# Linformer attention and gated FFN on one core: constants counted and transposed on VectorE instead of iotas on GpSimd, the broadcast library loaded behind the first loads

## The chip, the cores and the metric

One core of one Trainium2 chip. The metric is the device time of one execution in microseconds (us). Engines are called TensorE (PE in the profile), VectorE (DVE), ScalarE (ACT), Pool (GpSimd) and SP (SyncE). "PEld" is TensorE's weight load. The granted clock is the share of TensorE's full clock that the profile records as allowed; 0.5 is called the half clock below.

## The reference, cut to what matters

```python
k_proj = einsum('ks,bhsd->bhkd', E, k)            # B=8, H=8, S=1024, D=64, 64 projected keys
v_proj = einsum('ks,bhsd->bhkd', F, v)
attn   = softmax(q @ k_proj^T / 8)
x      = (attn @ v_proj), heads side by side      # 8192 x 512
out    = (sigmoid(x @ w_gate) * (x @ w_val)) @ w_out   # d_ff = 1536
```

Inputs are float32; the kernel loads all but E and F as bf16, casting in the DMA.

## The kernel before

Pool issues the large loads. The order of its work, with the iotas between the loads (shapes cut):

```python
def start_loads():
    # SP: E and F, 256 KB each
    load_k(0)                                    # Pool: K of batch 0, 1 MB written
    pool(iota(col_i), w=["col_i"]); pool(iota(row_i), w=["row_i"])
    load_q_half(0, 0); load_v(0)
    pool(iota(pat_i)); pool(iota(eight_i)); pool(iota(pat4_i))
    load_w(0); load_w(1); load_q_half(0, 1); load_w(2); load_w(3)

def constants():                                 # VectorE
    copy(col_f, col_i); copy(row_f, row_i)       # int32 -> float32
    identf = (col_f == row_f); ident = ...       # identity, float32 and bf16
    half, low, negm, dsel8, bsel8, bsel, dsel    # small masks, from col_i, row_i and the patterns
```

The head of the program, in TensorE's order. `busy(n)` are n filler matmuls that feed nothing. They are meant to keep the clock up; its mean was 1.0 in every run of before, but that the fillers do it is not shown.

```python
start_loads(); constants()
project_consts()              # transposes E and F with identf, 8 matmuls
busy(56)
project(0, 0, ...)            # K of batch 0 times E; waits for K
keep_k; turn_k(whole)
qt(0); qt(1); sc(0); sc(1); den()    # waits for q's first half; scores, exp, denominators
project(1, 1, ...)            # V of batch 0 times F; waits for V
keep_v; busy(8); bc(0); busy(4); xo(0); bc(1); xo(1); busy(10)   # xo: attention times V
load_q(1); load_k(1); load_v(1); load(wO)        # Pool: batch 1 and w_out
# then the dense FFN matmuls with the attention of the next batch in between;
# SP transposes q of batch 1 by four DMA transposes
```

Later (from batch 2 on), Pool spreads the reciprocals with `partition_broadcast`, which lies in another Pool library than iota: the trace of before has MODIFY_POOL_CONFIG at the first iota's line (2.33 us) and again at the broadcast's (110.5 us).

The softmax here doesn't subtract the row's maximum and nothing guards it: scores larger than these inputs give would overflow.

## Time and profile before

| | before |
|---|---|
| median of the first runs | 580.79 us (580.11 to 581.54, 4 runs) |
| all runs of before, over the study | 579.88 to 582.35 us |
| span of the profiled run | 578.0 us |
| TensorE busy | 555.5 us, 96% |
| first TensorE work | 15.48 us |
| first attention-times-V matmul (`xo`) | 30.37 us |
| dense FFN matmuls from | 33.46 us |

TensorE is near full use in all but the first 33 us, so the head is what can still be shortened. The prediction shows the lines that say so.

### The profile page before, as it was taken

Reading aid. Unit: us, or ns where it says so; the run is one execution under the profiler, and the core shown is the slowest. Engines: PE = TensorE matmul, PEld = TensorE weight load, DVE = VectorE, ACT = ScalarE, POOL = GpSimd, SP = SyncE. Lnnn points to the kernel's source line nnn. Section 1 sums busy time; section 2 is a strip of 40 time slices with the busy share of each in tenths; the row PEclk is TensorE's granted clock in tenths of the full one; section 3 lists DMA queues with packets and bytes.
Section 4 is the critical chain, followed back from the end, with each engine's and each line's share of the span. In section 5 each row is a group of like instructions: output and inputs, shape, how many; then the busy total and the mean of one; then the engine's idle time right before and its main releaser. Section 6 shows DMA issues by size and latency. Waiting matters only on the chain.

```text
span 578.0 us, 7834 instructions
## 1 busy us (share of the span) xinstructions
PE 555.5 (96%) x3110; PEld 252.1 (44%) x3110; DVE 246.4 (43%) x381; ACT 175.1 (30%) x317; POOL 101.5 (18%) x139
## 2 busy tenths in 40 slices
PE   0899999999999999999999999999999999999997
PEld 0644434544444444444444444444445444444443
DVE  0446355335443356235363354433562353633332
ACT  0355443352223422333223522234223332222220
POOL 1800010102600053000810026000520008000000
PEclk9999999999999999999999999999999999999999
DMA  6999979892576047650696125771311011100002
GB/s 109 160 203 200 186 125 194 150 195 58 108 148 119 37 65 134 127 90 36 111 173 104 44 57 108 148 119 37 75 56 45 21 38 38 37 36 19 36 37 91
DMA packets 74212, 56.01 MB, mean 97 GB/s; under 512 B 34528, under 2 KB 65760, under 8 KB 74176
## 3 DMA queue, kind: packets, MB, share of 16 engines
q0 software_dynamic: 31776, 29.89, 33.7%
q1 hardware_dynamic: 42400, 25.63, 17.5%
q8 instruction: 24, 0.39, 0.3%
q14 instruction: 12, 0.10, 0.1%
HBM read 60.29 MB, written 16.78 MB: 133 GB/s over the span
## 4 chain that ended last, share of the span: by engine, by line
PE 94%; issue 2%; DVE 2%; ACT 1%; POOL 0%; POOLq 0%; DVEq 0%
PE pF L218 85%; PE pA L218 9%; DVE rden L715 1%; ACT eT L222 0%; DVE xT L606 0%; ACT qT L222 0%; POOL KV L236 0%; DVE rden L553 0%; DVE vpD L464 0%; DVE identf L323 0%; DVE rhl L725 0%; DVE ost L878 0%; DVE hT L851 0%; DVE rhi L723 0%; ACT kp L222 0%
## 5 line engine op out<-in xcount | busy, mean ns | idle before, releaser
L851 DVE SCALAR_TENSOR_TENSOR hT<-sig,pF 128x512 bf16<-128x512 f32 x192 | 130.9, 685 | 203.3 <-PE pF L218 155.8
L222 ACT ACTIVATE sig<-pF 128x512 f32<-128x512 f32 x192 | 114.8, 599 | 315.9 <-PE pF L218 312.9
L218 PE MATMUL pF<-xT,wG 128*128 128x512 bf16 x768 | 198.6, 380 | 0.6 <-ACT rb L222 0.3
L218 PE MATMUL pF<-xT,wV 128*128 128x512 bf16 x768 | 198.2, 379 | 0.2 <-DVE xT L606 0.2
L218 PE MATMUL pF<-wO,hT 128*128 128x512 bf16 x720 | 165.4, 380 | 0.0
L218 PEld LDWEIGHTS pF<-xT,wV 128*128 128x128 bf16 x768 | 75.1, 98 | 90.9 <-issue 0.6
L218 PEld LDWEIGHTS pF<-xT,wG 128*128 128x128 bf16 x768 | 72.1, 98 | 94.2 <-issue 11.8
L760 POOL PARTITION_BROADCAST rb<-rrow x96 | 70.8, 798 | 219.3 <-DMA rrow<-rden 213.9
L218 PEld LDWEIGHTS pF<-wO,hT 128*128 128x128 bf16 x720 | 69.1, 98 | 87.3 <-issue 5.8
L878 DVE TENSOR_SCALAR ost<-pF 128x512 f32<-128x512 f32 x60 | 41.5, 691 | 94.0 <-PE pF L218 94.0
L222 ACT ACTIVATE eT<-pA 128x512 bf16<-128x512 f32 x63 | 32.7, 603 | 10.2 <-PE pA L218 10.2
L785 DVE TENSOR_TENSOR xT<-pA,rb 128x512 bf16<-128x512 f32 x56 | 34.7, 681 | 0.0
L715 DVE RECIPROCAL rden<-pA 128x128 f32<-128x128 f32 x28 | 23.7, 909 | 0.0
L236 POOL DMA_DIRECT2D KV<-in_k_dram x8 | 7.5, 937 | 82.4 <-PE pF L218 80.4
L236 POOL DMA_DIRECT2D KV<-in_v_dram x8 | 7.2, 895 | 75.0 <-PE pA L218 75.0
L218 PE MATMUL pA<-identf,EF 128*128 128x128 f32 x8 | 1.9, 421 | 15.5 <-DVE half L331 15.5
L218 PE MATMUL pA<-KV,EFT 128*64 128x256 bf16 x240 | 14.6, 274 | 0.0
L218 PEld LDWEIGHTS pA<-KV,EFT 128*64 128x64 bf16 x240 | 12.5, 110 | 3.1 <-issue 3.0
L222 ACT ACTIVATE kpd<-pA 128x512 bf16<-128x512 f32 x6 | 3.6, 597 | 28.4 <-PE pA L218 28.4
L218 PE MATMUL pA<-eT,vpD 64*64 64x512 bf16 (+1 forms) x136 | 10.4, 370 | 0.3 <-DVE vpD L464 0.3
L218 PE MATMUL pA<-qT,kpD 64*64 64x512 bf16 (+1 forms) x140 | 10.4, 367 | 0.3 <-ACT qT L222 0.3
L222 ACT ACTIVATE vpD<-pA 64x256 bf16<-64x256 f32 x28 | 10.5, 375 | 0.5
(74 smaller groups left out, 109.1 us busy)
## 6 DMA issues: line engine op xcount, KB each, us to landing
out_dram<-ost SPq DMA_DIRECT2D x64, 256.0 KB, 2.0
KV<-in_k_dram POOLq DMA_DIRECT2D x8, 1024.0 KB, 10.7
KV<-in_v_dram POOLq DMA_DIRECT2D x8, 1024.0 KB, 11.3
Qb<-in_q_dram POOLq DMA_DIRECT2D x7, 1024.0 KB, 15.2
wO<-in_moe_w_out_dram POOLq DMA_DIRECT2D x1, 1536.0 KB, 44.5
Qb<-in_q_dram POOLq DMA_DIRECT2D x2, 512.0 KB, 10.3
wG<-in_moe_w_gate_dram POOLq DMA_DIRECT2D x2, 512.0 KB, 18.3
wV<-in_moe_w_val_dram POOLq DMA_DIRECT2D x2, 512.0 KB, 20.1
```

The costliest lines, as they stand in the source:

```text
L218: return add("PE", lambda e: e.matmul(o, lhsT, rhs, **kw), r=r, x=[("bank", b)])
L222: return add("ACT", lambda e: e.activation(o, i, func, scale=scale), r=r, w=w, x=x)
L236: add("POOL", lambda e: e.dma_start(o, i), r=r, w=w, dma=sem)
L715: lambda e, cc=cc: e.reciprocal(rden[:, cc], bank[bk][:, cc]),
L760: lambda e, n=n, i=2 * rnd + c, j=j, parts=parts: e.partition_broadcast(rb[0:parts, n, :], rrow[32 * j : 32 * j + 1, i, :], channels=parts),
L785: lambda e, r=r, g=g, n=n, bk=bks[g]: e.tensor_tensor(xT[s][:, r, :, 256 * g : 256 * g + 256], bank[bk][:, :].rearrange("p (f c) -> p f c" ...
L851: lambda e: e.scalar_tensor_tensor(hT[blk % 2][:, m, :], sg[:, :], 1.0, bank[pv][:, :], ALU.add, ALU.mult,),
L878: lambda e: e.tensor_scalar(o[:, :], bank[pb][:, :], 0.5, None, op0=ALU.mult),
```

## The change

The intent is to have nothing of Pool's library code in front of the loads. Column numbers are built on VectorE by doubling (0, then +1, +2, +4 ...), row numbers by one transpose on VectorE of patterns 32 columns wide and adding 0, 32, 64, 96 (four memsets on Pool). The iotas go. The library with `partition_broadcast`, which was brought in by itself ahead of the first broadcast (at 110.5 us, the broadcast at 140.23), is asked for right behind the load of `wO`. The diff, cut to its core:

```diff
             load_k(0)                # four memsets of `quad` now stand ahead of it
-            pool(lambda e: e.iota(col_i[:, :], [[1, P]], channel_multiplier=0), w=["col_i"])
-            pool(lambda e: e.iota(row_i[:, :], [[1, 1]], channel_multiplier=1), w=["row_i"])
             load_q_half(0, 0)
             load_v(0)
-            ... (iotas of pat_i, eight_i, pat4_i)
 ...
         def constants():
-            dve(lambda e: e.tensor_copy(col_f[:, :], col_i[:, :]), ["col_i"], ["col_f"])
-            dve(lambda e: e.tensor_copy(row_f[:, :], row_i[:, :]), ["row_i"], ["row_f"])
+            dve(lambda e: e.memset(count[:, 0:1], 0.0), [], ["count"])
+            for i in range(7):
+                n = 1 << i
+                dve(tensor_scalar(count[:, n : 2 * n], count[:, 0:n], float(n), None, op0=ALU.add), ...)
+            dve(tensor_copy(pats[:, 0, :], count[:, 0:32]), ...)   # and three more patterns
+            dve(e.transpose(rows, pats), ["pats"], ["rows"])
+            dve(tensor_tensor(row_f, rows[:, 0, 0:1], quad, ALU.add), ...)
 ...   (dsel and dsel8 from twelve small pieces instead of four; bsel, bsel8, negm read `rows`)
         load(wO[:, :, :], moe_w_out.rearrange("(m p) c -> p m c", p=P), ["wO"], "wO")
+        spread_library = [ the first library that has InstPartitionBroadcast ]
+        pool(lambda e: e.load_library(spread_library))
```

## The prediction

> **What bounds the kernel now.** I read the page first, then the chain that ended last over the first 36 us, then the landing of each transfer, then the first use of each transferred tile. The page:
>
> ```profile
> span 578.0 us, 7834 instructions
> PE 555.5 (96%) x3110; PEld 252.1 (44%) x3110; DVE 246.4 (43%) x381; ACT 175.1 (30%) x317; POOL 101.5 (18%) x139
> PE   0899999999999999999999999999999999999997
> ```
>
> TensorE is busy in all but one slice of 14.45 us: the first reads 0. By TensorE's groups from 33 us to the end it idles about 1.4 us (0.9 of it one wait for `rhl`). So steady-state savings on other engines are worth nothing; the head before 33.46 us, where the dense FFN matmuls begin, is the only place this change can gain. The chain there (start, us, what):
>
> ```profile
> 1.24 1.01 POOL KV L236
> ...
> 2.33 0.03 POOLq L295
> ...
> 2.39 11.57 issue
> 13.96 0.24 POOL col_i L295
> ...
> 14.55 0.78 DVE identf L323
> ...
> 15.48 1.94 PE pA L218 x8
> 17.42 3.86 PE pF L218 x56
> 21.28 1.04 PE pA L218 x16
> ...
> 29.80 0.44 DVE vpD L464
> 30.23 0.14 issue
> 30.37 0.57 PE pA L218 x9
> ...
> 33.42 0.05 issue
> ```
>
> The reader should see a hole of 11.57 us between K's load and the first iota. The trace names the two Pool sequencer entries at 2.33 and 2.36 us MODIFY_POOL_CONFIG: the library with iota is being brought in. Everything after it in Pool's order waits too: the identity (so TensorE), but also every further load, because Pool issues them. The landings (issue time from Pool's timeline plus the last column, us from issue to landing):
>
> ```profile
> KV<-in_k_dram POOLq DMA_DIRECT2D x1, 1024.0 KB, 11.1
> EF<-in_F_dram SPq DMA_DIRECT2D x1, 256.0 KB, 4.2
> ...
> KV<-in_v_dram POOLq DMA_DIRECT2D x1, 1024.0 KB, 10.6
> ...
> wG<-in_moe_w_gate_dram POOLq DMA_DIRECT2D x1, 256.0 KB, 10.4
> ```
>
> F: 1.38+4.2 = 5.6 us. K: 1.24+11.1 = 12.35. First half of Q: 14.24+5.8 = 20.1. V: 15.33+10.6 = 25.9. First gate weights: 16.86+10.4 = 27.3. K sat landed for 8.9 us before its projection at 21.28.
>
> [...] The gap ends 1.6 us after K landed, so the load may also wait for the transfer under way; this profile cannot tell. [...] a q transpose issued at 50.00 us, beside the load stream, takes 11.9 us; the one at 72.24, when the stream is over, 3.0. [...]
>
> **The change, part by part.**
>
> *Five iotas and the library in front of them leave Pool.* 11.57 us of load, plus 0.23+0.12 us and some 0.65 us of later iotas in Pool's order. Added in front of K are four memsets; the four at 0.24 us start about 0.03 apart and last 0.10, so K issues some 0.15 us later: landing about 12.5. Pool's remaining issues (0.75 to 1.1 us each) follow at once: q's first half at about 2.4, wO, the last, near 14.5 instead of 26.33.
>
> *Constants on VectorE.* A small operation lasts 0.13 to 0.15 us (rows `half`, `low_i`); a dependent one starts about 0.04 us after its predecessor, estimated 0.18 per step. Memset plus seven doublings: 1.45; four patterns, which overlap: 0.5; [...] row_f 0.18; identf 0.78+0.12 to TensorE. Sum 3.5 us. VectorE can begin near 0.7 us (ScalarE's and SP's first work starts at 0.72), so the identity is ready at about 4.2, against 15.4. F lands at 5.6 and now starts TensorE. The rest (two halves, twelve `dsel` pieces at about 0.15, two `bsel` at 0.47) ends near 8.5, while the first denominators are due after 17. The later use of a pattern column for `negm` costs the same.
>
> *TensorE's head.* Transposes of E and F 5.6 to 7.5 us, 56 warming matmuls to 11.4, then K's projection waits for K: 12.5 instead of 21.28. That would be worth 8.8 us. But the wait now belongs to the transfers, and these gain less than the 11.9 us by which their issue moves: K's own stream was running until 12.35, so only the empty gap in the stream is saved. Once running, a quarter MB lands each 1.3 to 1.4 us (gate and value chunks at 27.3, 28.5, 30.95, 32.1 us; then 0.5 MB per 2.6). Behind K, q's half lands at 12.5+2.65 = 15.1, V at 15.1+5.3 = 20.4 (before: 25.9, so 5.5 earlier), first weights 21.8 and 23.1.
>
> K projection, copy, transposes of kp take 12.5 to 14.4; q's half lets its transposes begin at about 15.0 (23.19 before, 8.2 gained). Scores, exp, denominators end at 27.68-8.2 = 19.5. V's projection then waits for V: 20.4 instead of 27.59, ends 21.45; the two VectorE copies of vpD take 0.9, to 22.35; TensorE's fillers and first broadcast (29.36 to 30.09 before) end at about 22.6. So xo begins at about 22.65 instead of 30.37: 7.7 us gained. FFN weights (23.1) are there before it starts at 25.75.
>
> *Further down,* needs move by 7.7 and landings by 5.5, so each must have had 2.2 us in hand. Gate chunk 2 lands 30.95 for 36.79: kept. q's other half 34.7 for 38.5: kept. V of batch 1 62.0 for about 65.9, wO 70.8 for 74.8: kept. The tightest is q's fourth transpose for batch 1:
>
> ```profile
> 72.24 1.23 SPq L624 DMA_TRANSPOSE qT<-Qb  x1
> ...
> qT<-Qb SPq DMA_TRANSPOSE x1, 3.0
> ...
> 77.45 0.63 PE L218 MATMUL pA<-qT,kpD 64*64 64x512 bf16 x8
> ```
>
> It lands at 75.28; the second half of the matmuls at 77.45 uses it from about 77.7: 2.4 us in hand, 2.2 needed. I allow 0.1 us for a small stall.
>
> *The broadcast library.* Before, Pool loaded it by itself at 110.5 us (MODIFY_POOL_CONFIG, line 760), unseen ahead of the first broadcast at 140.23, which waited for a DMA. Now it starts near 15.5 us; Pool's next order is K of batch 2, at 75.98 before (bound by the transpose landing at 75.28). Even a 12 us load, or one that waits for the stream's end at 65 and takes some us more, costs that load a few us of the 19 between its landing (86.5) and its use at 105.3. Zero.
>
> Sum: -7.7 + 0.1 = -7.6; 581.43 - 7.6 = 573.8 us, 1.3% less.
>
> **The rivals.**
> 1. *Everything moves by the full hole.* TensorE's first work goes from 15.48 to 5.6: 9.9 us at most, time 571.5. Against it: K's landing at 12.35 is not moved by the change, and V's comes behind it. Only if K's stream is being slowed by the library load (142 GB/s in 4 to 12 us, against 207 later) does it come near.
> 2. *Transfers take the wait over completely.* If the stream gains only the empty stretch (12.35 to about 16.4, some 4 us plus the restart), or the transposes for batch 1 slip by interleaving differently, the gain is 5 to 6 us: 575.5 to 576.5. For it: 2.4 us in hand is little. Against it: they hang on the same stream and should move with it.
> 3. *The library load has only moved.* If loading behind the stream blocks Pool until the stream has drained and for 12 us after, K of batch 2 issues at about 77 instead of 70 and still has over 15 us. If it also held up transfers under way, the head would lose up to its own length: about 581. Against it: K landed during the first load, V of batch 3 around the second.
> 4. *VectorE's chain is the new start.* Twice my 3.5 us puts the identity at 7.7, first matmul 2.1 later, end of the fillers at 13.5: 1 us past K, and V's later wait absorbs most of it. About 574.5.
>
> **Range and chances.** The main claim, a hole replaced by transfers already measured, is firm; its size lies between the stream's 5.5 and the compute's 8.8. Runs of before spread 1.4 us. So 573.8, from 571.3 to 576.6. Faster by over 2% would need 11.6 us, more than the 9.9 that the landing of F allows: 2%. Slower by over 2% needs a stall of 19 us that nothing here suggests: 1%.
>
> **What would show it.** Right: no empty stretch on Pool between K's and q's issue; first TensorE work at 5.5 to 6; K projection at 12 to 13, released by the K transfer; V's projection at 20 to 20.8, released by V; dense matmuls from about 25.7; after that the same busy TensorE. Wrong, and in which step: identity after 5.6 us (VectorE's chain); K landing clearly off 12.5 (rival 1 or a slower stream); TensorE idle near 66 to 70 us for qT, or near 57 for KV (rival 2); the load of K for batch 2 after 90 us (rival 3)[...].

Passages are cut: one was the term for the transpose in VectorE's chain; the chain's 3.5 us were summed with it, and the terms that are left come to 3.03. The forecast's own sum, 7.6 us gained and 573.8 us, rests on V's landing, not on the identity.

## The result, and the profile after

The changed kernel takes 572.83 us (median of 4 runs, 572.16 to 573.38) against 580.79. The ratio is 0.9862, 95% interval 0.9843 to 0.9881. Ratios here are the mean time of one kernel's fast runs over that of the other's of the same rounds, so not quite the ratio of the medians that are quoted. That is 1.4% faster, far clear of noise. The prediction was 573.8 us.

The page of the changed kernel; compare its first TensorE slices (0 and 8 before):

```profile
span 571.1 us, 7787 instructions
...
PE   5799999999999999999999999999999999999997
```

The timeline of the changed kernel's head: start, us, engine, line, operation, and in brackets the idle time before it and what ended it.

```profile
0.72 0.56 POOL L288 MEMSET quad<- 32x1 f32 x4 [0.29 <-POOLq L981]
1.34 1.02 POOL L228 DMA_DIRECT2D KV<-in_k_dram  x1
2.36 0.88 POOL L228 DMA_DIRECT2D Qb<-in_q_dram  x1
3.23 0.88 POOL L228 DMA_DIRECT2D KV<-in_v_dram  x1
3.35 0.31 DVE L334 STREAM_TRANSPOSE rows<-pats 128x128 f32<-128x128 f32 x1
3.90 0.29 DVE L348 TENSOR_SCALAR identf<-count,row_f 128x128 f32<-128x128 f32 x1
5.54 1.94 PE L210 MATMUL pA<-identf,EF 128*128 128x128 f32 x8 [5.54 <-DMA EF<-in_F_dram]
7.27 5.16 PE L210 MATMUL pF<-ident 128*128 128x128 bf16 x56
13.38 1.06 PE L210 MATMUL pA<-KV,EFT 128*64 128x256 bf16 x16 [0.94 <-DMA KV<-in_k_dram]
16.03 1.07 PE L210 MATMUL pF<-ident,Qb 128*128 128x128 bf16 x16 [0.67 <-DMA Qb<-in_q_dram]
21.13 1.06 PE L210 MATMUL pF<-KV,EFT 128*64 128x256 bf16 x16 [0.56 <-DMA KV<-in_v_dram]
23.33 0.41 PE L210 MATMUL pA<-eT,vpD 64*64 64x256 bf16 x8
```

The hole in Pool is gone: q follows K at once. The identity is ready at 4.19 us and TensorE's first work waits for F. From there three steps of the head are each released by a transfer in this profile: K's projection, q's transposes and V's projection. The transfers have taken over the wait. (In the repeat, `after_again`, K landed at 12.09 us and its projection waited until 12.54 for the end of the 56 fillers instead.) Their landings, from the list of DMA issues of the changed kernel (last column: us from issue to landing):

```profile
KV<-in_k_dram POOLq DMA_DIRECT2D x1, 1024.0 KB, 12.0
...
Qb<-in_q_dram POOLq DMA_DIRECT2D x1, 512.0 KB, 13.6
...
KV<-in_v_dram POOLq DMA_DIRECT2D x1, 1024.0 KB, 17.8
```

So K lands at 13.3 us (12.35 before), q's half at 16.0 (20.1) and V at 21.1 (25.9). `xo` starts at 23.33 instead of 30.37, the unbroken dense matmuls at 26.44 instead of 33.46: 7.0 us gained in the head of these two profiles.

The chain that ended last now runs, further down, through the DMA transposes of q for batch 1:

```profile
44.35 11.52 DMA qT<-Qb
...
57.16 10.98 DMA qT<-Qb
...
68.16 3.04 DMA qT<-Qb
...
71.34 0.41 PE pA L210 x4
```

The fourth transpose lands at 71.20 (75.28 before, where nothing waited for it). TensorE now waits for it, 0.5 us. Part of that is taken back, since a wait for `rhl` (the reciprocals of the softmax denominators, prepared on VectorE) a few us later falls from 0.9 to 0.4 us.

### The profile page after: what moved, and what is told of

It reads as the page before. It is cut to its first block, busy times and chain, and to the rows that moved or that the text cites. A ratio compares the mean times of both kernels' runs of the same rounds, so it can differ in the third digit from the quotient of the medians.

```text
span 571.1 us, 7787 instructions
## 1 busy us (share of the span) xinstructions
PE 551.9 (97%) x3054; PEld 253.6 (44%) x3110; DVE 248.1 (43%) x392; ACT 175.0 (31%) x317; POOL 100.4 (18%) x138
## 4 chain that ended last, share of the span: by engine, by line
PE 85%; DMA 10%; POOL 2%; DVE 1%; issue 1%; SPq 0%; DVEq 0%; POOLq 0%
PE pF L210 78%; PE pA L210 7%; DMA Qb<-in_q_dram 6%; DMA qT<-Qb 4%; DVE rden L698 1%; POOL wG L228 1%; POOL wV L228 1%; POOL KV L228 0%; POOL Qb L228 0%; SPq L607 0%; DVE rhl L708 0%; DVE ost L861 0%; DVE hT L834 0%; DVE rhi L706 0%; POOL quad L288 0%
## 5 line engine op out<-in xcount | busy, mean ns | idle before, releaser
L210 PE MATMUL pF<-xT,wV 128*128 128x512 bf16 x743 | 195.6, 379 | 2.2 <-DVE xT L589 0.9
L210 PE MATMUL pF<-xT,wG 128*128 128x512 bf16 x743 | 193.2, 379 | 3.1 <-issue 2.4
L210 PEld LDWEIGHTS pA<-KV,EFT 128*64 128x64 bf16 x240 | 12.5, 110 | 4.1 <-issue 3.0
L210 PE MATMUL pA<-wO,hT 128*128 128x512 bf16 x47 | 10.5, 379 | 0.1
## 6 DMA issues: line engine op xcount, KB each, us to landing
wO<-in_moe_w_out_dram POOLq DMA_DIRECT2D x1, 1536.0 KB, 48.9
```

Source lines behind the costliest of these rows:

```text
L210: return add("PE", lambda e: e.matmul(o, lhsT, rhs, **kw), r=r, x=[("bank", b)])
```

## The experiments

Twelve kernels ran; all gave correct results.

### The size of the gain, and the explicit library load

`after_again` is the changed kernel, unaltered.

> The changed kernel unaltered, to size the gain. Theory (the head gains what the closed gap in the load stream gives, and the rest follows rigidly): the two profiles differ by 6.9 us in span, so 6.9 us. Rival (something beyond the head gains another us, as the first timing of 8.0 us suggests): 8 us. A ratio of 0.988 speaks for the first, 0.986 for the second.

Measured: 572.76 us (571.86 to 573.28), ratio 0.9858 (0.9836 to 0.9879). The gain is about 8 us; the 6.9 us between the profiles is too small because before's profile was its fastest run. The first theory fell as a size, though no further saving beyond the head had to be found. What makes before's own spans scatter by 2.4 us is not shown.

`lib_auto` leaves the explicit request out:

```diff
-        pool(lambda e: e.load_library(spread_library))
```

> The explicit library load is left out; the library is then brought in by itself before the first broadcast, after some 104 us. Theory (where the load lies behind the head it is hidden, at 17 us as at 105 us): within 0.5 us of the changed kernel, about 573. Rival (the explicit load is part of the gain): slower by several us, with a visible wait before the first broadcast near 133 us.

Measured: 572.78 us, ratio 0.986 (0.9843 to 0.9877). The explicit load is worth nothing, as expected. In the trace the first broadcast starts 0.09 us after the last increment of the semaphore of the DMA that it waits for, here as in the changed kernel; before, 0.13.

### Which part of the change does it

`iota_late` is the kernel before, with the loads of q and V ahead of the iotas: loads early, identity late.

```diff
             load_k(0)
-            pool(iota col_i); pool(iota row_i)
             load_q_half(0, 0)
             load_v(0)
+            pool(iota col_i); pool(iota row_i)
             pool(iota pat_i); ...
```

> The kernel before with its iotas, but the loads of q's first half and V issued ahead of them: loads early, identity late. Theory (TensorE cannot start without the identity, so early loads alone give nothing): with a library load of fixed length 11.6 us, iota at about 16, K projection near 23 instead of 21.3, V waiting no more; time about 581 to 583. If the library load also waits for the transfers under way (V would land near 20 to 21): iota near 22 and time about 588. Rival (the loads alone are the gain): about 574.

Measured: 581.67 us, ratio 1.0016 (0.9993 to 1.0038). Its Pool timeline:

```profile
3.13 0.88 POOL L236 DMA_DIRECT2D KV<-in_v_dram  x1
16.40 0.23 POOL L297 IOTA col_i<- 128x128 int32 x1 [12.39 <-issue]
```

V landed at 20.8 us and the iota did not wait for it; in `one_iota`, below, the iota starts at 12.23 us, ahead of K's landing at 12.38. So in neither run did the library load wait for the transfers under way. Early loads without the identity gave nothing: `xo` starts at 32.3. The identity is even a little later here than before (iota at 16.40 instead of 13.96).

`one_iota` is the reverse: the changed kernel, early identity, but one dead iota where the old ones were.

```diff
             load_k(0)
+            pool(lambda e: e.iota(dead_i[:, :], [[1, 1]], channel_multiplier=1), r=[quad...], w=["dead_i"])
             load_q_half(0, 0)
```

> The changed kernel plus one iota into a tile that nobody reads, between K's load and q's: the early identity stays, the loads behind K wait for a library function again. Theory (the wait is paid at the first call of a library function, so this iota brings it back to the loads): iota near 14, q's half lands near 20, V near 26; TensorE then waits for q and V; dense matmuls near 31, time about 578.5. Rival (the early identity alone is the gain): about 573.

Measured: 578.88 us (575.82 to 578.97), ratio 0.9948 (0.9925 to 0.997). Pool's timeline:

```profile
12.23 0.13 POOL L293 IOTA dead_i<- 128x1 int32 x1 [9.88 <-issue]
```

TensorE's waits (in total, times, longest):

```profile
PE pF L211 <- DMA Qb<-in_q_dram: 3.9, 1, 3.9
PE pF L211 <- DMA KV<-in_v_dram: 2.0, 1, 2.0
```

TensorE stands ready and waits for q and V. All four runs also lost the clock in part of the head (mean 0.985 to 0.994 of full; 0.50 from 15.6 to 29.2 us in the profile), so some of the loss is the clock's. An early identity alone, with the clock lost, brings about 3 of the 8 us; the run that lost least of it, 575.82 us, lies 5.6 below before's median, so without that loss it may be worth more. The two halves do not add: early loads alone 0, early identity alone about 3, both 8. Each was worth its full share only when the other did not hold the head.

### What holds Pool: the call, the load, or this library

`lib_behind_k` puts the broadcast library's load where the iota library's was.

```diff
             load_k(0)
+            pool(lambda e: e.load_library(spread_library))
             load_q_half(0, 0)
```

> Constants on VectorE as changed, but the broadcast library loaded right behind K's load, where iota's was. Theory (the loads behind the library are what matters, and the load itself holds Pool): q's first half issues near 14 us again and lands near 20, V near 26, dense matmuls from about 31 instead of 26.4, time about 578.5, so only 2 us of the gain stay. Rival 1 (the early identity is the gain): about 573. Rival 2 (Pool pays only when a library function is called, not for loading): q issues at 2.5 us, about 573.

Measured: 572.74 us, ratio 0.9859 (0.9842 to 0.9875). My theory fell: this load held nothing: q's order came 0.17 us after the end of K's.

```profile
2.53 0.91 POOL L228 DMA_DIRECT2D Qb<-in_q_dram  x1 [0.17 <-issue]
```

Either a load holds Pool only until a call of its code (rival 2), or the two libraries differ. `std_behind_k` asks for the iota library in the same place, and calls no iota:

```diff
             load_k(0)
+            pool(lambda e: e.load_library(library_config.standard))
             load_q_half(0, 0)
```

> The changed kernel with the iota library (not the broadcast library) asked for right behind K's load, and no iota called. Theory (loading that library holds all of Pool's later orders, DMA orders too, for some 10 us): q's first half issues at 12 to 14 us, dense matmuls near 32, one time near 579 as with one dead iota. Rival (only a call of a library function waits): q issues at 2.5 us, time about 573.

Measured, one look: 577.62 us.

```profile
12.17 1.07 POOL L228 DMA_DIRECT2D Qb<-in_q_dram  x1 [9.81 <-issue]
```

So the load of the iota library itself held Pool's next order, here a DMA order, for 9.7 us after the second MODIFY_POOL_CONFIG (2.47 us). No call was made. (A part of the lost time may be the clock's again: its mean was 0.991.) `lib_first` asks for the broadcast library ahead of everything:

```diff
         def start_loads():
+            pool(lambda e: e.load_library(spread_library))
```

> The changed kernel with the broadcast library asked for ahead of all of Pool's work, memsets and K's load. Theory (the broadcast library does not hold DMA orders, whatever its place; only the iota library did): K issues near 1.4 us, time about 573. Rival (any load that comes ahead of the first DMA order holds it, as iota's did for 7.4 us): K issues near 8 us, time about 579 to 580.

Measured, one look: 573.21 us, K issued at 1.40 us with no hole. For this library the place did not matter; that of iota, in `std_behind_k`, held. One rival is left: in both runs the broadcast library is the first that the program asks for, and whether it was in place already at the start is not tested. Where it was asked for behind the iota library (before, `one_iota`, `std_behind_k`, `iota_prefetch`), Pool's next order came only 30 to 52 us later, so a hold would not have shown.

`iota_prefetch` is the kernel before with the iota library asked for first and the iotas behind the weights.

```diff
+            pool(lambda e: e.load_library(library_config.standard))
             load_k(0)
-            (iotas)
             load_q_half(0, 0); load_v(0); load_w(0); ... load_w(3)
+            (iotas)
```

> The kernel before, with its iota library asked for as Pool's first order, then K, q, V and weights issued, and the iotas behind them. Theory (loading runs beside Pool's DMA orders and only a call waits for it, about 11.6 to 12.3 us after the request): first iota near 12.5 to 13, first matmul near 14, K projection near 20, time about 580. Rival (the call itself brings the code in, however early the request was): iota near 23, time about 588.

Measured, one look: 584.25 us. Both theories fell on K's issue, which neither had expected to be held:

```profile
8.27 1.20 POOL L236 DMA_DIRECT2D KV<-in_k_dram  x1 [7.84 <-issue]
...
17.99 0.36 POOL L303 IOTA col_i<- 128x128 int32 x1
```

The iota itself then waits for nothing, since the library came in before K's order. Asking early, ahead of the DMA orders, did not hide this load; the change leaves it out altogether. From the second MODIFY_POOL_CONFIG to the next order it took 7.4 us with none of Pool's transfers running, 9.7 to 11.6 beside K's transfer, and 12.3 beside K, q and V. Why it took longer beside transfers is not shown.

### What limits the changed kernel

In the profiles there is a simple regularity, found afterwards. Let X be the start of the first `xo` matmul and T the landing of the fourth q transpose of batch 1.

| profile | X | T | X+547.6 | T+499.9 | span |
|---|---|---|---|---|---|
| before | 30.37 | 75.28 | 578.0 | 575.2 | 578.0 |
| changed | 23.33 | 71.20 | 570.9 | 571.1 | 571.1 |
| after_again | 22.10 | 70.54 | 569.7 | 570.4 | 570.5 |
| lib_auto | 22.41 | 71.31 | 570.0 | 571.2 | 571.2 |
| lib_behind_k | 22.77 | 70.81 | 570.4 | 570.7 | 570.7 |
| lib_first | 23.06 | 71.48 | 570.7 | 571.4 | 571.4 |
| one_iota | 29.59 | 75.77 | 577.2 | 575.7 | 577.2 |
| iota_late | 32.27 | 69.83 | 579.9 | 569.7 | 579.9 |
| std_behind_k | 28.18 | 74.51 | 575.8 | 574.4 | 575.8 |
| iota_prefetch | 34.72 | 75.82 | 582.3 | 575.7 | 582.3 |
| q1_late | 24.04 | 69.54 | 571.6 | 569.4 | 571.8 |
| q1_early | 24.77 | 71.82 | 572.4 | 571.7 | 572.4 |
| warm_head | 23.91 | 69.75 | 571.5 | 569.6 | 571.5 |
| ef_pool | 25.38 | 70.82 | 573.0 | 570.7 | 573.9 |

The span is the larger of the two sums (547.6 is taken from before, 499.9 from the changed order), within 0.2 us except in the last row, where the clock stayed at half beyond X (0.50 from 19.6 to 29.85 us). Before, the head ruled by 2.8 us. In the changed order the two are within 1.2 us of one another, and T rules in all five profiles that keep the order and the queues of the loads and the free Pool (changed, after_again, lib_auto, lib_behind_k, lib_first). X itself hangs on one landing: in those five profiles and `warm_head` it comes 2.25 us behind the last increment of V's load (2.6 in `lib_auto`), and 3.5 to 4.0 us where the clock was at half between the two (`one_iota`, `std_behind_k`, `q1_late`, `q1_early`, `ef_pool`).

Two experiments were to move T.

`q1_early` loads q of batch 1 ahead of the last weights:

```diff
-        WCH = (0, 256, 512, 1024, 1536)
+        WCH = (0, 256, 512, 1024, 1280, 1536)
 ...
         load_q(1)
+        load_w(4)
         load_k(1)
```

> The changed kernel with the last quarter MB each of gate and value weights loaded behind q of batch 1 instead of ahead of it, so that q's DMA transposes begin some 2.6 us earlier. Theory (the end of the changed kernel is set by the landing of the fourth q transpose, 499.9 us before the end of the span in all four profiles of this form): the fourth transpose lands near 69.5 instead of 70.5 to 71.3, TensorE's wait for qT falls from 0.5 to 1.1 us to nothing, span about 570 or a little less, 0.5 to 1.2 us faster than the changed kernel. Rival (the head alone sets the end, the wait for qT is absorbed later): no change, 572.8; or slower if the weights now come late.

Measured: 573.79 us (571.88 to 575.83), ratio 0.9871 (0.985 to 0.9892). Not faster; T came at 71.82, no earlier, though q landed at 41.8 instead of 43.1 to 44.4. `q1_late` does the opposite:

```diff
-        load_q(1)
         load_k(1)
+        load_q(1)
```

> The converse: q of batch 1 loaded behind K of batch 1, about 5 us later. Theory: the transposes start near 49.5, share less with the load stream, and the fourth lands 1 to 4 us later, at 72 to 75; the span is that landing plus 499.9, so 572 to 575, time 574 to 577. Rival (the head sets the end): 572.8 still.

Measured: 573.07 us (572.71 to 573.59), ratio 0.9861 (0.9845 to 0.9877). q landed later, at 48.9, and T earlier, at 69.54. So my account of T, that it follows q's landing, is wrong. TensorE's waits in 60 to 80 us, first of `after_again`, then of `q1_late`:

```profile
PE pA L210 <- DMA qT<-Qb: 1.1, 1, 1.1
PE pA L210 <- DVE rhl L708: 0.4, 1, 0.4
```

```profile
PE pA L210 <- DVE rhl L708: 0.9, 1, 0.9
```

The wait for qT is gone in `q1_late`, yet the time is not better, because its head was later. That had two causes: V landed at 20.5 (19.9 in `after_again`), and TensorE's clock fell. The busy times by stretch (columns: us, busy of PE, PEld, DVE, ACT, POOL, granted clock, DMA share, GB/s), first of `q1_late`, then of `after_again`:

```profile
17.00:21.00 4.00, 2.15 (x29) 1.36 (x27) 1.53 (x3) 1.59 (x4) 0.00 (x0) 1.00 1.37 199
21.00:24.40 3.40, 3.40 (x40) 2.20 (x35) 0.85 (x2) 1.55 (x4) 0.00 (x0) 0.50 1.45 196
```

```profile
17.00:21.00 4.00, 3.08 (x42) 1.92 (x43) 1.54 (x3) 1.89 (x5) 0.00 (x0) 1.00 1.35 201
21.00:24.40 3.40, 3.11 (x55) 1.96 (x54) 2.58 (x5) 2.83 (x6) 0.00 (x0) 1.00 1.45 196
```

From V's projection to `xo` took 3.5 us at the half clock (20.54 to 24.04) and 2.2 at the full one (19.90 to 22.10).

`warm_head` joins three edits: the order of `q1_late`, 33 more fillers in waits of the head, the memsets behind K's load.

```diff
-        load_q(1)
         load_k(1)
+        load_q(1)
 ...
         keep_k(bk, 0)
+        busy(6)
 ...
         qt(1)
+        busy(6)
         sc(0); sc(1)
-        den()
+        busy(4)
+        den(3)            # three fillers between its groups
+        busy(8)
```

> The changed kernel with three small edits: K of batch 1 loaded ahead of q of batch 1 (there the fourth q transpose landed 1 to 1.8 us earlier), 33 more filler matmuls in the waits of the head so that the clock is not lost in a window of it (it was at half for 3.4 us in three of the five runs whose order of loads is that of the changed kernel or nearly), the four memsets behind K's load. Theory (the landing of the fourth transpose and a lost clock window are what takes back part of the head's gain): no wait for qT, no half-clock window before 570 us, dense matmuls from 25.2 to 26, span 569.7 to 570.6, time 571.3 to 572.2. Rival (the head is set by the landings of K, q and V alone, which scatter by 1.2 us from run to run): 572.8 as the changed kernel.

Measured: 572.61 us (571.82 to 573.37), ratio 0.9855 (0.9831 to 0.9879). No half-clock window in any of its four runs (mean clock 1.0 in each) and no wait for qT, as expected, but in its profile K landed at 13.1 and V at 21.7, and X was 23.91. The rival holds for the time: what remains is set by the landings, and these scatter; X is again V's landing plus 2.25 us. In both runs in which T came earlier, X came later, so that T sets the end of the changed kernel is read from the table and not shown by an experiment. No version clearly beats the changed kernel.

`ef_pool` asks where that scatter comes from:

```diff
-                add("SP", ... dma_start(EF[rows, :], src[:, :]) ...)
+                add("POOL", ... dma_start(EF[rows, :], src[:, :]) ...)
```

> The changed kernel with E and F loaded through Pool's queue ahead of K instead of through SP's beside it. In the profiles of the changed order the sixteen increments of K's semaphore come over 1.4 to 3.0 us, and V lands between 19.8 and 21.7 us with the same laggards. Theory (the laggards come from two queues sharing the engines in the first 5 us): K's increments now come within 1 us, K near 12, V within 19.3 to 20; time about 572. Rival (they come from elsewhere): K's increments over 1.4 us or more as before; time 573, since E and F land about a us later but TensorE waits for K anyway.

Measured: 572.83 us (572.04 to 575.7), ratio 0.985 (0.9833 to 0.9866). (Landed means here: with the last of the sixteen increments of the load's semaphore. In the changed kernel's profile V's last came 2.2 us behind its eighth.) K's increments came over 1.4 us and V's over 2.4; V landed at 21.4. The rival holds, as far as one profile tells: V's laggards came without two queues at the start too. Where they come from stays open. For K, 1.4 us is the least of the range before (3.0 in the changed kernel's profile). Its two slowest runs, 575.7 and 574.71 us, are the ones with a mean clock of 0.991 and 0.993; the four with 1.0 lie between 572.04 and 572.84. The runs that lost the clock took 1.9 to 3.7 us more than the others here.

## Why the prediction was right, step by step

- **The hole in Pool is the cost, and it holds the loads as well as the identity.** Right. Taking either half back (`one_iota`, `iota_late`) costs 6 and 9 us against the changed kernel (in the first, with a mean clock of 0.985 to 0.994, part of the 6 may be the clock's). The prediction left open whether the library load also waits for the transfer under way; it did not (`iota_late`: iota at 16.40 us, V landed at 20.8; `one_iota`: 12.23, K landed at 12.38).
- **VectorE's chain, 3.5 us, identity near 4.2.** Measured 4.19, with errors that cancel: a doubling step took 0.24 us and not 0.18, the float32 identity 0.29 and not 0.78. The transpose took 0.31. The start waits for F at 5.54. The 56 fillers, put at 3.9 us and their end at 11.4, took 5.2 and ended at 12.4: mis-sized, and hidden behind K in this profile, not in the repeat.
- **Transfers take over the wait; the stream gains less than its issue.** Right in kind, and small errors in each landing: K 12.5 predicted and 13.3 measured, q 15.1 and 16.0, V 20.4 and 21.1, `xo` 22.65 and 23.3. All lie inside the scatter of profiles of the same order: V 19.8 to 21.1. Pool's last order came at 15.9 us, not 14.5, because V of batch 1 first waited 2.3 us for K's projection; the stream stayed full (mean DMA share 1.30 from 10 to 20 us), so it seems to have cost nothing.
- **The fourth transpose, 0.1 us of stall.** Mis-sized. I moved its landing by the stream's 5.5 us, which is 69.8; it came at 71.2, and TensorE waited 0.5 us (1.1 in the repeat). Net of the shorter wait for `rhl` this cost 0.1 us in the first profile (7.0 gained at `xo`, 6.9 in the span) and 0.8 in the repeat. In the five profiles of the changed order it lands 6.3 to 6.6 us behind the last landing of the stream (`wO`), before 4.5, but in `ef_pool` 4.5 too. Why is not settled; both attempts to explain it by q's landing failed.
- **The broadcast library, zero.** Right (`lib_auto`, `lib_behind_k`, `lib_first`). Rival 3, that its load would hold Pool as the first one did, did not happen where it was the first library asked for (Pool's next order 0.17 us after the end of K's in `lib_behind_k`, K issued at 1.40 us in `lib_first`).
- **The sum.** Predicted 7.6 us gained, measured 8.0 in the first runs. The profiles show 6.9, and since the prediction was worked out on before's profile, that is the number to hold against it: 0.7 too much, since `xo` gained 7.0 and not 7.7. The rest of the measured 8.0 is before's profile having been its fastest run, by up to 2.4 us of span, which the prediction did not reckon with. That 7.6 lies so near to 8.0 is in part luck.
- **The lost clock.** It did not occur in the changed kernel's first four runs (mean clock 1.0 in each), but in others of the same order (0.997 in one run of the repeat).

## What to carry to other kernels

Look for the first Pool instruction that needs a library to be brought in: a gap on Pool that ends in no wait (11.57 us here) may be holding the loads queued behind it, not only its own result. When the hole is closed, the next limit is whatever was hidden in it; read the landings before predicting the size, and check the slack of every later use: here the needs moved by 7.0 us (`xo`) and the landings by less (V 4.8, the fourth q transpose 4.1). Where two limits lay within 1.2 us of each other, as here, relieving one showed nothing.
